# Softmax weighting with V as the stationary operand in four column tiles, row sums spread by DMA

## The chip, the cores and the metric

The kernel runs on one core of a Trainium2 chip. The metric is the device time of one execution in microseconds (us). Engines: PE (TensorE, matrix products into PSUM), DVE (VectorE), ACT (ScalarE), POOL (GpSimd) and SP, which here only issues DMAs.

## The reference, cut to what matters

```python
xn = layernorm(x)                                # x: 2048 x 640, bf16
q, k, v = xn @ wq, xn @ wk, xn @ wv              # 32 heads of 20, in 4 segments of 512 rows
for s in range(4):
    p = softmax(qs @ ks.T * 20 ** -0.5 + causal mask)
    a_dot = p @ vs
    a_mem = (phi(qs) @ M) / (phi(qs) @ z + 1e-6)      # memory of the earlier segments
    o = g * a_mem + (1 - g) * a_dot                   # g = sigmoid(beta), one per head
    M, z = M + phi(ks).T @ vs, z + phi(ks).sum()
s = concat(o) @ wo
glu = (sigmoid(xn @ w_gate) * (xn @ w_up)) @ w_down
out = x + s * silu(glu)
```

## The kernel before

The program is emitted segment by segment (n = 0 to 3), and each segment in 20 **slots**: four pairs of head groups (a group is 4 heads), five slots to a pair (`UNITS`). In a slot `scores` multiplies up to 512 columns of K by Q for 4 heads, in four row tiles of 32 partitions, into one PSUM tile `Sps`; ACT takes the exponential into `pt` (keys on partitions, queries along the row), POOL zeroes what lies over the diagonal. One slot later (two for the second half of unit 2) `weigh` multiplies by V.

`weigh` (L534) holds a 128x128 block of `pt` stationary and streams the 21 columns of one head's V: 20 values and a 1, so that column 20 of the result is the softmax's row sum. A group needs ten blocks times four heads, 40 matmuls, into one PSUM tile `A` (queries on partitions; one buffer, `ps_a`). After the group's last block DVE takes the reciprocal of the row sums (L553), multiplies it by 1 - g (L554) and multiplies the group into `od` (L556). At the start of the next segment `o_ready` adds the memory's part `om` (L468) and turns `od` by DMA transposes into `oT` (L475), which `o_proj` (L502) multiplies by Wo: five chunks of 128 rows. `mem_read` (L410 to L418) makes `om`.

The order of the work is written out by a planner. `at(time, cost, fn)` puts a task at a time that is counted in slots; `later` puts one behind the current task. The feed-forward part (`gate` L428, `up` L438, `down` L456) is a list `bulk`, from which `fill` takes as much as evens out the slots, with PE costs in us from `PASS` and the tasks' own. In a slot come `scores`, 0.45 of the slot's bulk, the due `weigh` passes, and the rest. The last four `down` passes are kept for the end, and in the tail `o_last` turns the last chunk on PE. All matmul results but `Sps` and `A` share three PSUM buffers (`ps_d`), which DVE or ACT empties. Each engine works in the order of emission, and so does SP with its DMAs: a DMA that waits holds all behind it. V, K, Q of the next segment (`v_tile` L360, `k_chunk` L289, `q_chunk` L321), the bound of the scores (`q_bound` L334, five matmuls of 32 columns in four column tiles) and the relays of K and Q through DRAM (L274, L310, L353) are tasks of the same planner, and so are the transposes of phi(K), `pkt` (L378).

Of the kernel before, what the change touches and what calls it, by code (L numbers as in the profile page):

```python
# [9 lines left out]
P = 128  # L10
S = 2048
D = 640
H = 32
DH = 20
VW = DH + 1
KR = DH + 4
NSEG = 4
# [36 lines left out]
FIRST = 0.45  # L54
PASS = [0.41, 0.41, 0.41, 0.2, 0.61]
R = NSLOT / 24
# [3 lines left out]
def kernel(  # L60
# [31 lines left out]
    Ks = [dpool.tile([D, L], BF, name=f"Ks{i}") for i in range(2)]  # L92
    Cs = [dpool.tile([4, H, L], BF, name=f"Cs{i}") for i in range(2)]

    ctx.enter_context(tc.manual_schedule(engines={ENG.PE, ENG.Activation, ENG.DVE, ENG.Pool, ENG.SP}))
# [24 lines left out]
    def empty(fn):  # L120
        pending.append((seq[0], fn))
        if not delay[0]:
            flush()

    def later(lag, fn, *a):
# [43 lines left out]

    def load_late(name, src):  # L170
        parts = src.shape[0] // P
        W[name] = cpool.tile([P, parts, D], BF, name=f"W{name}")
        nc.scalar.dma_start(W[name][:], src.rearrange("(f p) n -> p f n", p=P))

# [6 lines left out]
                            base=0, pattern=[[-1, P]], channel_multiplier=1)  # L181
    V = []
    for i in range(8):
        va = cpool.tile([P, H, VW], BF, name=f"va{i}")
        V.append(va)
    QT = [cpool.tile([P, 4, L], BF, name=f"QT{i}") for i in range(3)]
    KT = [cpool.tile([P, 4, L], BF, name=f"KT{i}") for i in range(3)]
    nInd = cpool.tile([P, DC, H], F32, name="nInd")
    BD = cpool.tile([P, DC, HW, VW], BF, name="BD")
    Mbd = cpool.tile([P, DC, HW, VW], BF, name="Mbd")  # L190

    def v_ones(a, b):
        for i in range(a, b):
            nc.gpsimd.memset(V[i][:, :, DH:VW], 1.0)

    def make_ind():
# [16 lines left out]

    gin = {}

    def gates():
# [185 lines left out]
    def mem_read(n, j, b):  # L402
        s = st[n]
        if j == 0 and b == 0:
            s["om"] = opool.tile([P, 4, D], BF, name="om", bufs=1)
        am = dtile([P, 16, VW], F32, "am")
        parts = [c for c in range(DC) if H0[c] < 16 * b + 16 and H1[c] > 16 * b]
        for i, c in enumerate(parts):
            lo, hi = max(H0[c], 16 * b), min(H1[c], 16 * b + 16)
            nc.tensor.matmul(am[:, lo - 16 * b:hi - 16 * b, :].rearrange("p h e -> p (h e)"),  # L410
                             lhsT=s["q5"][:, c, j * P:(j + 1) * P],
                             rhs=Mbd[:, c, lo - H0[c]:hi - H0[c], :].rearrange("p h e -> p (h e)"),
                             start=(i == 0), stop=True, skip_group_check=True)
        rm = opool.tile([P, 16], F32, name="rm", bufs=3)
        nc.vector.scalar_tensor_tensor(out=rm[:], in0=am[:, :, DH], scalar=1e-6,
                                       in1=gin["ginv"][:, 16 * b:16 * b + 16], op0=ALU.add, op1=ALU.mult)
        nc.vector.reciprocal(rm[:], rm[:])
        nc.vector.tensor_tensor(  # L418
            s["om"][:, j, b * HB:(b + 1) * HB].rearrange("p (h e) -> p h e", e=DH),
            am[:, :, 0:DH], rm[:].unsqueeze(2).to_broadcast([P, 16, DH]), op=ALU.mult)  # L420

# [42 lines left out]

    def o_add(n, j, c0, c1):
        o = st[n]["od"][:, j, c0:c1]
        if n >= 1:
            nc.vector.tensor_tensor(o, o, st[n]["om"][:, j, c0:c1], op=ALU.add)  # L468

    def o_turn(n, j, parts):  # L470
        if "oT" not in st[n]:
            st[n]["oT"] = fpool.tile([P, 4, DC, P], BF, name="oT", bufs=1)
        dst = st[n]["oT"][:, j, 0:parts, :]
        src = st[n]["od"][:, j, 0:parts * P]
        later(0.7, lambda: nc.sync.dma_start_transpose(dst, src))  # L475

    def o_ready(n, j, parts=DC):
        o_add(n, j, 0, parts * P)
        o_turn(n, j, parts)

    def o_last(n):
        po = dtile([P, 4, P], BF, "po")
        for j in range(4):
            nc.tensor.transpose(po[:, j, :], st[n]["od"][:, j, (DC - 1) * P:D], ident[:])
        nc.scalar.copy(st[n]["oT"][:, :, DC - 1, :], po[:])

# [8 lines left out]
    def o_proj(n, j, half):  # L495
# [5 lines left out]
        for c in range(DC):  # L501
            nc.tensor.matmul(sp[:], lhsT=s["oT"][:, j, c, :], rhs=W["o"][:, c, hs],  # L502
                             start=(c == 0), stop=(c == DC - 1))
# [29 lines left out]

    def weigh(n, pair, u, dg, pt):  # L534
        s = st[n]
        g = 2 * pair + dg
        first = (u, dg) in ((0, 0), (2, 1))
        if first:
            s["A"] = ps_a.tile([P, 4, 4, VW], F32, name="Aps")
        A = s["A"]  # L540

        mine = [(kb, c0) for (d, kb, c0, ncol) in UNITS[u] if d == dg]
        blocks = [(kb, c0 + (qb - kb) * P, qb) for (kb, c0) in mine for qb in range(kb + 1, 4)]
        blocks += [(kb, c0, kb) for (kb, c0) in mine]
        for (kb, off, qb) in blocks:
            for r in range(4):
                nc.tensor.matmul(A[:, qb, r, :], lhsT=pt[:, r, off:off + P],  # L547
                                 rhs=V[4 * (n % 2) + kb][:, 4 * g + r, :],
                                 start=first, stop=True, skip_group_check=True)
                first = False  # L550
        if (u, dg) in ((2, 0), (4, 1)):
            rd = opool.tile([P, 4, 4], F32, name="rd", bufs=3)
            nc.vector.reciprocal(rd[:], A[:, :, :, DH])  # L553
            nc.vector.tensor_tensor(rd[:], rd[:], gin["omg"][:, 4 * g:4 * g + 4].unsqueeze(1).to_broadcast([P, 4, 4]),  # L554
                                    op=ALU.mult)
            nc.vector.tensor_tensor(  # L556
                s["od"][:, :, 4 * g * DH:(4 * g + 4) * DH].rearrange("p q (r e) -> p q r e", e=DH),
                A[:, :, :, 0:DH], rd[:].unsqueeze(3).to_broadcast([P, 4, 4, DH]), op=ALU.mult)

# [13 lines left out]
    def startup():  # L573
# [33 lines left out]
        make_bd()  # L607
        v_ones(4, 8)
        take(1)
        relay(0, 0, Qs, QT)  # L610
# [5 lines left out]
        ln_stats(1, 1, 0, 1)  # L616
        gates()
        take(1)
        ln_norm(1, 0, 0)
# [13 lines left out]

    startup()
    at(6.8, 0, load_late, "d", B_w_down)
    at(10.2, 0, load_late, "o", A_wo)


    for n in range(NSEG):
        w = NSLOT * n  # L640
        m = n + 1
        if m < NSEG:
# [7 lines left out]
            for c in range(DC):  # L650
                at(w + R * (8.8 + 1.0 * c), 1.08, k_chunk, m, c)
                at(w + R * (13.8 + 1.1 * c), 1.08, q_chunk, m, c)
                if m + 1 < NSEG:
                    at(w + R * (12.8 + 0.85 * c), 0.0, phi, m, "k5", c)
                at(w + R * (18.3 + 0.8 * c), 0.0, phi, m, "q5", c)
# [7 lines left out]
            for i, cs in enumerate(([0, 1, 2], [3, 4])):  # L663
                at(w + R * (10.0 + 3.2 * i), 0.75 - 0.25 * i, m_update, n, cs)
        if n >= 1:
            for j in range(4):
                at(w + R * (1.1 + 0.3 * j), 0.0, o_ready, n - 1, j)
                at(w + R * (4.0 + 0.5 * j if j < 3 else 9.6), 0.0, xr_load, n - 1, j)
            for i in range(8):
                at(w + R * (5.4 + 1.1 * i), 0.68, o_proj, n - 1, i // 2, i % 2)  # L670
                at(w + R * (3.4 + 0.85 * i), 0.25, mem_read, n, i // 2, i % 2)

    for j in range(4):
        at(NSLOT * NSEG - 8 + 0.5 * j, 0.0, xr_load, NSEG - 1, j)
        at(NSLOT * NSEG - 0.9 + 0.2 * j, 0.0, o_ready, NSEG - 1, j, DC - 1)

# [10 lines left out]

    due, held = [], []
    for n in range(NSEG):
        st[n]["od"] = opool.tile([P, 4, D], BF, name="od")  # L690
        if n:
            bulk += [(1.09, fn, (n, f)) for f in range(FC) for fn in (gate, up)]
        bulk += [(1.64, down, (n, j, h)) for j in range(4) for h in range(2)]
        keep = 4 if n >= NSEG - 2 else 0

# [20 lines left out]
        for slot in range(NSLOT):  # L716
            pair, u = divmod(slot, NU)
            now = NSLOT * n + slot
            share = max(level - fixed[slot], 0.0)
            pt = scores(n, pair, u)  # L720
            delay[0] = True
            goal += FIRST * share
            fill(now + 0.45, (tasks,))
            for w in due:
                weigh(*w)
            delay[0] = False
            flush()
            while first and first[0][0] < now + 1.0:
                run_task(first)
            due, held = held, []  # L730
            due.append((n, pair, u, UNITS[u][0][0], pt))
            if u == 2:
                held.append((n, pair, u, 1, pt))
            goal += (1.0 - FIRST) * share
# [5 lines left out]

    cost, fn, a = bulk.pop(0)
    fn(*a)
    for w in due:
        weigh(*w)
    drain()
    n = NSEG - 1
    for j in range(4):
        o_add(n, j, (DC - 1) * P, D)
    for i, (cost, fn, a) in enumerate(bulk):
        if i == len(bulk) - 1:  # L750
            o_last(n)
        fn(*a)
    for j in range(4):
# [32 lines left out]
```

## Time and profile before

| | |
|---|---|
| median of 3 runs | 341.0 us (340.95 to 342.18) |
| the profiled execution | 342.2 us, span 340.5 us |
| instructions | 8352 |
| weighting, L547 | 1280 matmuls, 44.6 us busy; as many weight loads, 43.3 us |
| first scores of the four segments and of the last slot | 32.8, 103.1, 185.2, 260.2 and 321.0 us |
| DMA | 35.5 MB in 54725 packets, 104 GB/s on average |

A line of the page's groups reads: line, engine, operation, output<-inputs, shapes, count | busy us, mean ns of one | idle time of the engine before them and what ended it. A line of the timeline reads: start in us from the span's start, duration, engine, line, operation, count. The slices show the busy share in tenths, in 40 equal parts of the span. Matmuls are pipelined: PE's pace is read from starts, not from durations.

### The profile page before, as it was taken

Reading aid. Unit: us, or ns where it says so; the run is one execution under the profiler, and the core shown is the slowest. Engines: PE = TensorE matmul, PEld = TensorE weight load, DVE = VectorE, ACT = ScalarE, POOL = GpSimd, SP = SyncE. Lnnn points to the kernel's source line nnn. Section 1 sums busy time; section 2 is a strip of 40 time slices with the busy share of each in tenths; the row PEclk is TensorE's granted clock in tenths of the full one; section 3 lists DMA queues with packets and bytes.
Section 4 is the critical chain, followed back from the end, with each engine's and each line's share of the span. In section 5 each row is a group of like instructions: output and inputs, shape, how many; then the busy total and the mean of one; then the engine's idle time right before and its main releaser. Section 6 shows DMA issues by size and latency. Waiting matters only on the chain.

```text
span 340.5 us, 8352 instructions
## 1 busy us (share of the span) xinstructions
PE 330.1 (97%) x3402; PEld 186.8 (55%) x3402; DVE 223.6 (66%) x533; ACT 225.7 (66%) x236; POOL 111.5 (33%) x157
## 2 busy tenths in 40 slices
PE   8999899999999999999999999999999999999995
PEld 7543455545664565554466456554456655544673
DVE  6375366769786577778758867885655677633455
ACT  3652797688886666477686765565887775786730
POOL 6645232222245222332235312323222323233214
PEclk9999999999999999999999999999999999999999
DMA  7953984665822621045720461042220521110032
GB/s 237 339 182 108 329 130 87 229 212 125 185 74 37 120 74 45 19 137 93 218 72 2 87 127 40 21 154 80 79 69 3 84 74 40 58 60 2 3 62 77
DMA packets 54725, 35.53 MB, mean 104 GB/s; under 512 B 28576, under 2 KB 54688, under 8 KB 54688
## 3 DMA queue, kind: packets, MB, share of 16 engines
q1 hardware_dynamic: 52480, 32.23, 36.5%
q10 hardware_dynamic: 2208, 2.79, 2.5%
q8 instruction: 26, 0.43, 0.5%
q14 instruction: 11, 0.09, 0.1%
HBM read 20.19 MB, written 8.39 MB: 84 GB/s over the span
## 4 chain that ended last, share of the span: by engine, by line
PE 83%; DMA 6%; DVE 6%; ACT 2%; POOL 1%; issue 1%; SPq 1%; DVEq 0%; ACTq 0%; POOLq 0%
PE up L438 14%; PE gp L428 14%; PE yp L456 11%; PE Aps L547 8%; PE Sps L522 6%; PE psk L289 6%; PE sp L502 6%; PE psv L360 6%; PE psq L321 6%; DMA Cs<-cb 2%; DMA Wu<-in_B_w_up_dram 2%; PE wps L571 2%; DMA xnT<-xn 1%; PE dm L388 1%; DMA Qs<-q 1%; PE am L410 1%
## 5 line engine op out<-in xcount | busy, mean ns | idle before, releaser
L527 ACT ACTIVATE pt<-Sps 128x2048 bf16<-128x2048 f32 x80 | 150.2, 1877 | 28.9 <-PE Sps L522 26.1
L530 POOL TENSOR_SCALAR_AFFINE_SELECT pt<-pt 128x1024 bf16<-128x1024 bf16 (+1 forms) x80 | 75.7, 947 | 196.7 <-ACT pt L527 196.7
L428 PE MATMUL gp<-xnT,Wg 128*128 128x512 bf16 x240 | 59.7, 379 | 1.1 <-DMA Wg<-in_B_w_gate_dram 0.6
L438 PE MATMUL up<-xnT,Wu 128*128 128x512 bf16 x240 | 59.7, 380 | 0.2 <-DMA Wu<-in_B_w_up_dram 0.2
L456 PE MATMUL yp<-Wd,hT 128*128 128x320 bf16 x384 | 57.1, 299 | 0.0
L442 DVE SCALAR_TENSOR_TENSOR hT<-tg,up 128x512 bf16<-128x512 bf16 x48 | 32.7, 682 | 30.4 <-PE up L438 27.4
L431 ACT ACTIVATE tg<-gp 128x512 bf16<-128x512 f32 x48 | 28.6, 597 | 35.9 <-PE gp L428 35.9
L547 PEld LDWEIGHTS <-pt 128*128 128x128 bf16 x1280 | 43.3, 96 | 14.7 <-DVE od L556 1.4
L547 PE MATMUL Aps<-va,pt 128*128 128x21 bf16 x1280 | 44.6, 173 | 0.9 <-DVE od L556 0.7
L456 PEld LDWEIGHTS <-hT 128*128 128x128 bf16 x384 | 35.3, 97 | 15.3 <-issue 2.4
L438 PEld LDWEIGHTS <-Wu 128*128 128x128 bf16 x240 | 21.2, 97 | 24.6 <-issue 3.5
L522 PE MATMUL Sps<-QT,KT 24*128 24x128 bf16 (+3 forms) x512 | 32.6, 301 | 1.4 <-ACT pt L527 0.7
L428 PEld LDWEIGHTS <-Wg 128*128 128x128 bf16 x240 | 21.0, 97 | 22.9 <-issue 2.1
L461 DVE SCALAR_TENSOR_TENSOR aa<-t,yp 128x320 bf16<-128x320 bf16 x32 | 15.2, 482 | 19.5 <-ACT t L459 19.3
L360 PE MATMUL psv<-Wv,xnT 128*128 128x320 bf16 x160 | 26.4, 300 | 0.8 <-ACT tg L431 0.5
L459 ACT ACTIVATE t<-yp 128x320 bf16<-128x320 f32 x32 | 14.0, 437 | 19.2 <-PE yp L456 18.0
L502 PE MATMUL sp<-Wo,oT 128*128 128x320 bf16 x160 | 25.9, 300 | 0.0
L522 PEld LDWEIGHTS <-KT 24*128 24x128 bf16 x512 | 9.5, 92 | 27.0 <-issue 25.9
L321 PE MATMUL psq<-xnT,Wq 128*128 128x512 bf16 x100 | 24.3, 380 | 0.0
L289 PE MATMUL psk<-xnT,Wk 128*128 128x512 bf16 x100 | 24.3, 380 | 0.0
L504 DVE SCALAR_TENSOR_TENSOR aa<-aa,sp 128x320 bf16<-128x320 bf16 x32 | 15.5, 485 | 8.5 <-PE sp L502 8.4
L553 DVE RECIPROCAL rd<-Aps 128x16 f32<-128x16 f32 x32 | 8.1, 254 | 16.4 <-PE Aps L547 16.4
(74 smaller groups left out, 333.6 us busy)
## 6 DMA issues: line engine op xcount, KB each, us to landing
KT<-Ks SPq DMA_DIRECT2D x32, 80.0 KB
QT<-Qs SPq DMA_DIRECT2D x32, 80.0 KB
xr<-in_A_x_dram SPq DMA_DIRECT2D x15, 160.0 KB
out_dram<-xr SPq DMA_DIRECT2D x15, 160.0 KB
xt<-in_A_x_dram SPq DMA_DIRECT2D x6, 320.0 KB
Wg<-in_B_w_gate_dram SPq DMA_DIRECT2D x3, 640.0 KB
Wu<-in_B_w_up_dram SPq DMA_DIRECT2D x3, 640.0 KB
Wd<-in_B_w_down_dram ACTq DMA_DIRECT2D x1, 1920.0 KB
```

Of the source, the lines that this page charges most:

```text
L289: nc.tensor.matmul(ps[:], lhsT=W["k"][:, k, c * P:(c + 1) * P], rhs=s["xnT"][:, k, :], start=(k == 0), stop=(k == DC - 1))
L321: nc.tensor.matmul(ps[:], lhsT=W["q"][:, k, c * P:(c + 1) * P], rhs=s["xnT"][:, k, :], start=(k == 0), stop=(k == DC - 1))
L360: nc.tensor.matmul(ps[:], lhsT=s["xnT"][:, k, j * P:(j + 1) * P], rhs=W["v"][:, k, half * HB:(half + 1) * HB], start=(k == 0), stop=(k == ...
L428: nc.tensor.matmul(gp[:], lhsT=Wg[f // 4][:, k, fo:fo + P], rhs=s["xnT"][:, k, :], start=(k == 0), stop=(k == DC - 1))
L438: nc.tensor.matmul(ps[:], lhsT=Wu[f // 4][:, k, fo:fo + P], rhs=s["xnT"][:, k, :], start=(k == 0), stop=(k == DC - 1))
L442: empty(lambda: nc.vector.scalar_tensor_tensor(out=h[:], in0=tg[:], scalar=1.0, in1=ps[:], op0=ALU.add, op1=ALU.mult))
L456: nc.tensor.matmul(yp[:], lhsT=s["hT"][f][:, j * P:(j + 1) * P], rhs=W["d"][:, f, hs], start=(f == 0), stop=(f == FC - 1))
L502: nc.tensor.matmul(sp[:], lhsT=s["oT"][:, j, c, :], rhs=W["o"][:, c, hs], start=(c == 0), stop=(c == DC - 1))
L522: nc.tensor.matmul(Sps[:, r, c0:c0 + ncol], lhsT=kt[32 * r:32 * r + KR, gi, kb * P:(kb + 1) * P], rhs=qt[32 * r:32 * r + KR, gi, kb * P:L] ...
L527: nc.scalar.activation(pt[:], Sps[:], ACT.Exp, scale=SCALE)
L530: nc.gpsimd.affine_select(out=diag, in_=diag, compare_op=ALU.is_ge, fill=0.0, base=0, pattern=[[0, 4], [0, cnt], [1, P]], channel_multipli ...
L547: nc.tensor.matmul(A[:, qb, r, :], lhsT=pt[:, r, off:off + P], rhs=V[4 * (n % 2) + kb][:, 4 * g + r, :], start=first, stop=True, skip_grou ...
```

## The change

V becomes the stationary operand: 32 columns from a head's place in V (21 of its own, the rest of the next heads', or ones) in the column tile of that head, and `pt` is streamed, up to 512 columns at once, so a group has 16 matmuls in four column tiles. The result has the heads' values on partitions: partitions 32r to 32r+19 are head r's output, 32r+20 is its row sum, and the 11 others hold nothing of use. The passes come due two slots later (three for the second half of unit 2) and are emitted at the head of a slot, right before `scores`.

A whole group is copied from PSUM by one operation, into `oa` (groups 0 to 2) or `ob` (groups 3 to 7). `divide` sends the row sums through DRAM, so that they lie on 128 partitions, inverts them, multiplies by 1 - g (`oc`, made by `columns` with the masks of `make_sel`), sends them back through DRAM to 20 partitions a head (`rdb`), and `scale` multiplies. Groups 0 to 2 then go through DRAM (`spill`, `fill_holes`) into the 12 free partitions of each head in `ob`, so that Wo is needed in five chunks of 128 rows; Wo is put in that order through DRAM (`wo_gather`, `wo_load`), and `mem_read` writes `om` in that order too, with four multiplications for the first half, and transposes it by DMA. For the last two groups of the last segment `spread` copies the row sums to their partitions with a matmul by `sel`, and inverts 128x512 at once. Some tasks move in time.

```diff
-PASS = [0.41, 0.41, 0.41, 0.2, 0.61]
+PASS = [0.32, 0.21, 0.21, 0.21, 0.11]
+NA = 3
...
+    def wo_gather():
+        W["o"] = cpool.tile([P, DC, D], BF, name="Wo")
+        for r in range(4):
+            nc.sync.dma_start(Wx[r], wo_rows[r][:, 0:NA, :])
+
+    def wo_load(r):
+        nc.sync.dma_start(W["o"][32 * r:32 * r + DH, :, :], wo_rows[r][:, NA:NG, :])
+        nc.sync.dma_start(W["o"][32 * r + DH:32 * r + 32, :, :],
+                          Wx[r].rearrange("e g n -> (e g) n").rearrange("(c x) n -> x c n", c=DC))
...
+        lo = 4 * NA if b == 0 else 16
         nc.vector.tensor_tensor(
-            s["om"][:, j, b * HB:(b + 1) * HB].rearrange("p (h e) -> p h e", e=DH),
-            am[:, :, 0:DH], rm[:].unsqueeze(2).to_broadcast([P, 16, DH]), op=ALU.mult)
+            om[:].rearrange("p (h x) -> p h x", x=32)[:, lo - 4 * NA:16 * b + 16 - 4 * NA, 0:DH],
+            am[:, lo - 16 * b:16, 0:DH],
+            rm[:, lo - 16 * b:16].unsqueeze(2).to_broadcast([P, 16 * b + 16 - lo, DH]), op=ALU.mult)
+        if b == 0:
+            holes = om[:].rearrange("p (c r x) -> p r c x", c=DC, r=4)
+            for g in range(NA):
+                nc.vector.tensor_tensor(
+                    holes[:, :, :, DH + g::NA],
...
+            return
...
+        later(0.8, lambda: nc.sync.dma_start_transpose(dst, om[:]))
...
+    def divide(n, g0, g1, col, time):
...
+        def den_out():
+            for a, b in spans(g0, g1):
+                nc.sync.dma_start(Ds[:, a - g0:b - g0, :], rows_of(n, a, b)[DH::32])
+
+        def den_in():
+            nc.sync.dma_start(dn[:], Ds.rearrange("r g (k x) -> (r g k) x", x=16 * cnt))
+
+        def invert():
+            nc.vector.reciprocal(rc[:], dn[:])
+            nc.vector.tensor_scalar(rb[:], rc[:], oc[:, col:col + 1], None, op0=ALU.mult)
+
+        def rec_out():
+            nc.sync.dma_start(Rs.rearrange("r g (k x) -> (r g k) x", x=16 * cnt), rb[:])
+
+        def rec_in():
+            for r in range(4):
+                nc.sync.dma_start(rdb[32 * r:32 * r + DH, 0:cnt, :], Rs[r].partition_broadcast(DH))
+
+        def scale(a, b):
+            o = rows_of(n, a, b)
+            nc.vector.tensor_tensor(o, o, rdb[:, a - g0:b - g0, :], op=ALU.mult)
+
+        soon(time + 0.1, den_out)
+        soon(time + 0.75, den_in)
+        soon(time + 1.5, invert)
+        soon(time + 1.55, rec_out)
+        soon(time + 2.2, rec_in)
+        for g in range(g0, g1):
+            soon(time + 2.9 + 0.25 * (g - g0), scale, g, g + 1)
...
+    def fill_holes(n, c0, c1):
+        for r in range(4):
...
+            nc.sync.dma_start(st[n]["ob"][32 * r + DH:32 * r + 32, c0:c1, :], rows[:, c0:c1, :])
+
+    def spread(n, g, col):
+
+        o = st[n]["ob"][:, g - NA, :]
+        ps = dtile([P, L], F32, "dps")
+        nc.tensor.matmul(ps[:], lhsT=sel[:], rhs=o, start=True, stop=True)
+        nc.vector.reciprocal(ps[:], ps[:])
+        nc.vector.scalar_tensor_tensor(out=o, in0=o, scalar=oc[:, col:col + 1], in1=ps[:],
+                                       op0=ALU.mult, op1=ALU.mult)
...
+        for (d, kb, c0, ncol) in UNITS[u]:
+            if d != dg:
+                continue
             for r in range(4):
-                nc.tensor.matmul(A[:, qb, r, :], lhsT=pt[:, r, off:off + P],
-                                 rhs=V[4 * (n % 2) + kb][:, 4 * g + r, :],
-                                 start=first, stop=True, skip_group_check=True)
-                first = False
...
+                h = 4 * g + r
+                nc.tensor.matmul(A[32 * r:32 * r + 32, kb * P:L],
+                                 lhsT=Vw[4 * (n % 2) + kb][:, h * VW:h * VW + 32], rhs=pt[:, r, c0:c0 + ncol],
+                                 start=first, stop=True, skip_group_check=True, tile_position=(0, 32 * r))
+            first = False
...
+        (nc.scalar.copy if now >= NSLOT * NSEG else nc.vector.tensor_copy)(rows_of(n, g, g + 1).rearrange(
+            "p g n -> p (g n)"), A[:])
+        last = n == NSEG - 1
+        if g == 3:
+            divide(n, 0, 4, 0, now)
+            soon(now + 3.9, spill, n)
+        elif g == 7 and not last:
+            divide(n, 4, 8, 1, now)
+            soon(now + 0.3, fill_holes, n, 0, DC)
+            soon(now + 2.9, o_add, n, 0)
+        elif g == 5 and last:
+            divide(n, 4, 6, 2, now)
+            soon(now + 0.5, fill_holes, n, 0, 3)
...
+        elif g == 6 and last:
+            soon(now + 0.4, spread, n, 6, 3)
+            soon(now + 0.6, fill_holes, n, 3, 4)
+            soon(now + 0.95, o_add, n, 3)
...
-        keep = 4 if n >= NSEG - 2 else 0
+        keep = {NSEG - 2: 4, NSEG - 1: 5}.get(n, 0)
...
+            passes(now)
             pt = scores(n, pair, u)
+            due.append((now + 2, (n, pair, u, UNITS[u][0][0], pt)))
...
+    take(1)
+    passes(NSLOT * NSEG + 1)
     drain()
...
+    take(1)
+    spread(n, 7, 4)
+    fill_holes(n, 4, 5)
+    take(len(bulk))
+    o_add(n, 4)
     for j in range(4):
         for h in range(2):
             o_proj(n, j, h)
```

## The prediction

> **What bounds the kernel now.** I read the summary and the slices first: they say which engine could set the end.
>
> ```profile
> PE 330.1 (97%) x3402; PEld 186.8 (55%) x3402; DVE 223.6 (66%) x533; ACT 225.7 (66%) x236; POOL 111.5 (33%) x157
> PE   8999899999999999999999999999999999999995
> PEclk9999999999999999999999999999999999999999
> ```
>
> PE is busy in every slice and its clock is full. A busy PE need not be at its peak, so next comes the timeline of PE alone, where starts tell the pace.
>
> ```profile
> 162.83 0.75 PE L547 MATMUL Aps<-va,pt 128*128 128x21 bf16 x24
> 163.43 1.24 PE L428 MATMUL gp<-xnT,Wg 128*128 128x512 bf16 x5
> 164.60 0.40 PE L522 MATMUL Sps<-QT,KT 24*128 24x512 bf16 x4
> 164.93 1.25 PE L321 MATMUL psq<-xnT,Wq 128*128 128x512 bf16 x5
> ...
> 243.76 0.55 PE L547 MATMUL Aps<-va,pt 128*128 128x21 bf16 x16
> 244.24 0.60 PE L334 MATMUL cps<-aq,IK 128*32 128x512 bf16 x5
> 244.78 0.40 PE L522 MATMUL Sps<-QT,KT 24*128 24x128 bf16 x8
> 245.11 1.25 PE L438 MATMUL up<-xnT,Wu 128*128 128x512 bf16 x5
> ```
>
> Three things are read here. 24 weighting matmuls take 163.43 - 162.83 = 0.60 us, 25 ns each, and the next group follows at the same pace. Full 512-column matmuls are 0.216 us apart (five in 1.24, of which the last one's own 0.38 overlaps what follows). And each change of the array's shape costs something: from the first gp at 163.43, five of 0.216 end at 164.51, the scores start at 164.60; their 0.216 of streaming ends at 164.82, psq starts at 164.93. So some **0.095 us a change**. Beyond these paces PE's starts leave only some 5 us of stalls between 45 and 330 us, half of it next to weighting passes. So a nanosecond taken from PE is a nanosecond gained, unless another engine then holds it up. The timeline of the tail shows that there is no pause at the end to hide anything in: after the last scores at 321.02 one group follows the other until the output.
>
> ```profile
> 321.97 3.42 PE L456 MATMUL yp<-Wd,hT 128*128 128x320 bf16 x24
> 325.22 0.55 PE L547 MATMUL Aps<-va,pt 128*128 128x21 bf16 x16
> 325.63 3.42 PE L456 MATMUL yp<-Wd,hT 128*128 128x320 bf16 x24
> 328.88 0.39 PE L484 MATMUL po<-ident,od 128*128 128x128 bf16 x4
> 329.11 1.79 PE L456 MATMUL yp<-Wd,hT 128*128 128x320 bf16 x12
> 330.74 5.60 PE L502 MATMUL sp<-Wo,oT 128*128 128x320 bf16 x40
> ```
>
> Last, the groups by shape, for what VectorE will be asked to do.
>
> ```profile
> L553 DVE RECIPROCAL rd<-Aps 128x16 f32<-128x16 f32 x32 | 8.1, 254 | 16.4 <-PE Aps L547 16.4
> L224 DVE RECIPROCAL ginv<-gcol 128x32 f32<-128x32 f32 x1 | 0.3, 339 | 0.0
> L415 DVE SCALAR_TENSOR_TENSOR rm<-am,ginv 128x16 f32<-128x16 f32 x24 | 4.0, 168 | 2.1 <-PE am L410 2.1
> L323 DVE CAST q<-psq 128x512 bf16<-128x512 f32 x15 | 10.3, 688 | 8.0 <-PE psq L321 7.9
> L556 DVE TENSOR_TENSOR od<-Aps,rd 128x320 bf16<-128x320 f32 x32 | 15.7, 491 | 1.1
> ```
>
> **1. The weighting passes on PE: -13.2 us.** Before: 1280 matmuls x 25 ns = 32.0. After: for each of 32 head groups four chunks (512, 384, 256 and 128 columns), each as four matmuls in four column tiles. Whether such tiles run together is shown by cps: its first four matmuls lie in four column tiles with 512 columns, and all five have 0.60 us, which is one matmul's 0.39 and 0.21 more: the fifth, in the first one's tile, starts about 0.22 after the first. So the four cost what one does. A chunk costs columns/512 x 0.216 and about 0.01 for the staggered starts: 0.22 + 0.17 + 0.12 + 0.07 = 0.59 a group, 18.8 in all.
> The Trainium skill (TensorE: Matmul & The Clock Gate, Measured speedup vs the span model) gives 3.07x, not 4x, for four row tiles of 512 columns; by that the passes would take 32 x 1280 x 4 columns / 2.4 GHz / 3.07 = 22 us, an estimate, and 3.4 of the gain would go. The 0.22 us from first to fifth matmul speaks against it here.
>
> **2. One more change of shape in each slot: +7.8 us.** Before, the weighting had the bulk's 128*128 shape and went in without a seam (162.83 to 163.43). After, the slot begins bulk to column tiles, column tiles to row tiles, row tiles to bulk: three changes where there were two. The new one is column to row, and cps to Sps shows it: first cps 244.24, 0.43 for two rounds, Sps at 244.78, so 0.10 over. 80 slots x 0.095 = 7.6, and 0.2 for the last pass, which has no scores behind it. The two sel matmuls (0.43) replace four transposes (0.22): +0.2. PE's own work: **-13.2 + 7.8 + 0.2 = -5.2 us**.
>
> **3. VectorE gets more work and waits: +3.0 us.** Out: 32 x (0.254 + 0.257 + 0.491) = 32.1 us of L553 to L556, and the od additions, 7. In: 31 copies of 128x512 out of PSUM at 0.688 = 21.3; 30 products by rdb at 0.42 (the od addition of 128x512 has 419 ns) = 12.6; 15 additions of omT, 6.3; eight inversions of 64 or 32 columns, 0.7 each = 5.5; in 12 reads of the memory four small operations of some 0.25 for one of 0.49, +6; columns(), 2; the two wide reciprocals with their products, 8 (below). Net +22 us, some 4 in each segment. The windows view has VectorE busy 16.94 of 20 us at 139 to 159 and 16.31 of 20 at 178 to 198; there the two divisions of a segment fall (slots 11 to 15, and 1 to 5 of the next), each adding about 2.3: over 90%. VectorE runs in order, and now waits for DMAs: `invert` for dn, the products for rdb. Queued behind them are the evacuations of up, V and k that give PE its three ps_d buffers. A dependent DMA was issued 2.6 us after its source (Ks at 222.53, KT at 225.17), and four relays took 1.46 us to issue. So den_out, den_in, invert, rec_out and four rec_in take about 1.9 + 1.6 + 0.7 + 1.6 + 3 us from the copy's end to the product, where the plan has 2.9 slots of 3.9 us less the copy's 1.5: about even, until SP stands at a pkt transpose (L378 waited up to 3.6 us for VectorE, and issues for 1.2) ahead of rec_in. SP's load itself (20 issues of 0.4 in, four transposes out per segment) is small beside its idle time. Lower end: PE feels none of it and the 2.4 us that it lost around the old passes go, -2.4; upper end, six divisions with two waits of 0.7 each passed on whole, +8.5. I take +3.0, nearer to the lower end, since two free buffers cover 2 us of a stall. Startup: make_sel is some 5 us of POOL behind 30 us, where it waited 5.9 before its first mask at 36.5; nothing. Wo by a copy in DRAM: nothing, it is needed 80 us later.
>
> **4. The tail: +5.5 us.** The last two groups divide by `spread`: sel matmul, a reciprocal of 128x512, a product, four DMAs (fill_holes), an addition, then the projection's chunk. The trace has no such reciprocal. From 16 to 32 columns it rises by 85 ns and it stands 85 over the ordinary operation of 16: about 6.1 ns a column, so 0.16 + 512 x 6.1 = **3.3 us**; the other end is the copy of that shape, 0.69. I take 3.3. From the end P of the last passes: copy on ScalarE under one down pass (1.64); sel at P+1.9; behind that pass's evacuation VectorE starts the reciprocal at P+2.9, done P+6.2, product P+6.9, four DMAs 3.3 (1.46 of issue and the landing), P+10.2, addition P+10.6. PE has 1.64 + 0.3 + 3 x 1.64 + 0.54 (four of five chunks) = 7.4. It is 3.2 short. For group 6 the same 4.0 us of VectorE stand in slot 79 ahead of the down passes' evacuations, and o_add(3) then holds them again for its DMAs; one buffer is sel's, so PE runs about one pass further: some 2.3 lost. Ends: 0.6 with the short reciprocal; 9 if the rdb products of groups 4 and 5 (slots of 3.0 us there, a chain of 11) come late as well.
>
> **The sum.** The profiled execution has 342.2 us (span 340.5, 1.7 around it); the runs' median is 341.0, 1.2 less. 342.2 - 5.2 + 3.0 + 5.5 = 345.5, and as a median **344.3 us**, +1.0%. The bounds: -5.2 - 2.4 + 0.6 gives 334.0; -5.2 + 8.5 + 9 gives 353.3.
>
> **Rivals.**
> A, it pays: VectorE keeps up, and the tail's reciprocal is short or covered. For it: VectorE waits for PE 27 us before hT alone, and is nearly idle from 305 to 321 (5.51 of 16). Against: the slope of the two reciprocals. 341.0 - 5.2 - 0.5 + 1 = 336.3. Chance 0.27.
> B, a little of each, the gain and the tail cancel: 341 within 1.7. Chance 0.20.
> Forecast, 342.7 to 347.5: chance 0.33.
> C, slower by VectorE's waits for DMA: place, the rdb product at the end of a division's third slot; price, 0.7 to 1.5 us each time for 12 waits; it decides from a wait of over two PE tiles (2.2 us), when no free buffer is left. 341.0 - 5.2 + 8.5 + 5.5 = 349.8. Chance 0.12.
> D, a pause of PE in the tail slows its clock. In the empty start 40 matmuls of 128 columns took 4.45 us, 0.106 apart; po's four are 0.056 apart. A cold stretch as long as that first one loses 2.2 us: 344.3 + 2.2 = 346.5. The Trainium skill (TensorE: Matmul & The Clock Gate, HAM oscillation) has the clock halved after about 3.4 us of idleness; no run here shows that. The pauses worked out above are 1.5 to 3 us. Chance 0.06.
> E, the column tiles run one after another: 1280 x 4 x 32 columns at 0.216 per 512 are 69 us, +50: 394. cps speaks against it. Chance 0.02.
>
> **How the numbers follow.** Faster by over 0.5%: A, 0.27. Within 0.5% (about what this measurement can tell from no change): B, 0.20. Slower: the forecast, C, D and E, 0.53. The range leaves out the ends of A and of C, and E: 335.5 to 350.5.
>
> **What would show it.** Aps matmuls of 128*32 in fours, a 512 chunk 0.22 from the next (1); Sps 0.31 after the last Aps of 512 columns (2); idle time of VectorE put down to DMA dn and rdb, idle time of PE put down to VectorE in slots 12 to 15 (3); a RECIPROCAL of 128x512 at 3.3 us twice, and PE gaps of 1.5 to 3 us after 320 us (4). If that reciprocal takes under 1 us, the forecast falls to A; if the gaps stand in the body and not in the tail, C is right.

## The result and the profile after

The changed kernel takes 383.1 us (380.3 to 385.5) against 341.1 before: ratio 1.122, 95% interval 1.113 to 1.131. Forecast were 344.3 us and a range of 335.5 to 350.5. The direction was right, the size was not: 42 us instead of 3. In e4, e5 and e9 below one of each run's four executions was slow, and their times and ratios leave it out.

The summary and the clock's slices of the changed kernel (its slowest execution, 385.5 us, span 383.8 us) show the difference at once: PE is busy for 336.0 us against 330.1 before, but that is 88% instead of 97% of the span, and its clock now dips.

```profile
PE 336.0 (88%) x2599; PEld 166.3 (43%) x2632; DVE 241.4 (63%) x563; ACT 227.3 (59%) x236; POOL 114.8 (30%) x175
PE   8998996995989989998999989898999599969865
PEclk9999998897999999999999989999999899989899
```

The list of waits of the same profile (who waited for whom: total us, times, longest) says for what:

```profile
PE Aps L658 <- DVE ob L668: 11.9, 6, 4.1
DVE ob L565 <- DMA rdb<-Rs: 10.4, 3, 5.1
DVE oa L565 <- DMA rdb<-Rs: 9.1, 4, 4.1
PE Aps L658 <- DVE oa L668: 6.5, 4, 3.3
DVE k L326 <- DMA pkt<-k: 6.4, 1, 6.4
DVE rc L553 <- DMA dn<-Ds: 5.9, 2, 3.1
DVE ob L565 <- DMA xr<-in_A_x_dram: 5.0, 1, 5.0
```

L565 is `scale`, L553 `invert`, L668 the copy of a group out of PSUM. (The line with xr is rdb too: the wait ended at 301.26, and the transfer that `scale` needs came in beside xr.) VectorE stood 30 us before dn and rdb, and PE 18 us before copies that were behind. One such place follows, in the timelines of SP, VectorE and PE. (SPq is the issue of a DMA; Ds and Rs are the DRAM buffers of the row sums and of their inverses, Os that of the spilled groups.)

```profile
287.67 0.53 SPq L547 DMA_DIRECT2D Ds<-ob  x1
289.56 1.54 SPq L588 DMA_DIRECT2D ob<-Os  x4
291.14 0.36 SPq L550 DMA_DIRECT2D dn<-Ds  x1
295.02 0.34 SPq L557 DMA_DIRECT2D Rs<-rb  x1
296.46 1.42 SPq L561 DMA_DIRECT2D rdb<-Rs  x4
```

```profile
301.26 0.43 DVE L565 TENSOR_TENSOR ob<-ob,rdb 128x512 bf16<-128x512 bf16 x1 [4.96 <-DMA xr<-in_A_x_dram]
301.60 0.75 DVE L580 TENSOR_TENSOR ob<-ob,omT 128x512 bf16<-128x512 bf16 x2
302.27 0.68 DVE L668 CAST oa<-Aps 128x512 bf16<-128x512 f32 x1
```

```profile
295.86 1.25 PE L491 MATMUL gp<-xnT,Wg 128*128 128x512 bf16 x5
298.45 1.24 PE L501 MATMUL up<-xnT,Wu 128*128 128x512 bf16 x5 [1.34 <-ACT tg L494]
303.01 0.83 PE L658 MATMUL Aps<-pt,va 128*32 128x256 bf16 x8 [3.32 <-DVE oa L668]
303.78 0.61 PE L634 MATMUL Sps<-QT,KT 24*128 24x512 bf16 x4
```

The row sums leave at 287.67, and their inverses are usable at 301.26. VectorE waits 4.96 us in its order; the copy that empties `A` stands behind the waiting product and two additions, and the next pass needs `A`. PE starts no matmul from 299.3 to 303.0, and then a batch of 4 scores takes 0.61 us where it took 0.40: the clock has gone to half. A wait of VectorE of 1.92 us was enough for a pause of 4.12 us on PE, since the pass needed `A` before that wait began, and two operations on phi(K) stood between the product and the copy:

```profile
90.42 0.43 DVE L565 TENSOR_TENSOR oa<-oa,rdb 128x512 bf16<-128x512 bf16 x1 [1.92 <-DMA rdb<-Rs]
91.69 0.68 DVE L668 CAST ob<-Aps 128x512 bf16<-128x512 f32 x1
92.42 0.83 PE L658 MATMUL Aps<-pt,va 128*32 128x256 bf16 x8 [4.12 <-DVE ob L668]
```

The windows view, over stretches that begin in the pauses or just behind them, gives the clock (the column before the DMA share):

```profile
63.60:70.40 6.80, 5.50 (x23) 1.77 (x24) 4.13 (x7) 1.88 (x1) 0.42 (x1) 0.50 0.19 67
90.90:97.70 6.80, 5.28 (x24) 2.04 (x24) 5.21 (x12) 1.88 (x1) 0.68 (x1) 0.50 1.17 192
224.00:227.40 3.40, 3.35 (x16) 1.92 (x14) 3.30 (x12) 2.10 (x2) 0.84 (x1) 0.51 0.00 0
302.60:306.00 3.40, 2.99 (x19) 1.11 (x19) 3.30 (x10) 1.50 (x1) 0.00 (x0) 0.51 0.02 5
340.10:343.50 3.40, 3.40 (x9) 1.02 (x7) 0.33 (x1) 2.11 (x2) 0.68 (x1) 0.50 0.29 116
357.20:360.60 3.40, 3.40 (x15) 1.90 (x13) 3.37 (x5) 0.24 (x1) 0.07 (x1) 0.50 0.02 5
```

PE is busy for 23.9 of these 27.2 us at half clock; at full clock that work would take about half as long, so an estimate of 12 us is the clock's in this execution. Five of the six stretches follow a wait of a division. The first follows another pause: PE stood 3.14 us until 64.68 behind the copy of K, which waited 6.4 us for pkt (the list's fifth line). Where nothing waits, the passes do what was worked out. The next lines show PE in a quiet slot, then the tail: its first pause is still behind an rdb product (of groups 4 and 5), the other two belong to the tail's own division, with its reciprocal.

```profile
192.95 0.40 PE L658 MATMUL Aps<-pt,va 128*32 128x128 bf16 x8
193.28 0.40 PE L634 MATMUL Sps<-QT,KT 24*128 24x512 bf16 x4
193.61 3.43 PE L519 MATMUL yp<-Wd,hT 128*128 128x320 bf16 x24
...
356.83 0.38 PE L594 MATMUL dps<-ob,sel 128*128 128x512 bf16 x1 [2.72 <-DVE ob L668]
357.05 5.09 PE L519 MATMUL yp<-Wd,hT 128*128 128x320 bf16 x24
...
366.46 3.42 PE L519 MATMUL yp<-Wd,hT 128*128 128x320 bf16 x24 [1.67 <-DVE aa L524]
370.92 1.79 PE L519 MATMUL yp<-Wd,hT 128*128 128x320 bf16 x12 [1.04 <-DVE ob L596]
```

```profile
358.59 3.36 DVE L595 RECIPROCAL dps<-dps 128x512 f32<-128x512 f32 x1
```

### The profile page after: what moved, and what is told of

It reads as the page before. It is cut to its first block, busy times and chain, and to the rows that moved or that the text cites. A ratio compares the mean times of both kernels' runs of the same rounds, so it can differ in the third digit from the quotient of the medians.

```text
span 383.8 us, 6989 instructions
## 1 busy us (share of the span) xinstructions
PE 336.0 (88%) x2599; PEld 166.3 (43%) x2632; DVE 241.4 (63%) x563; ACT 227.3 (59%) x236; POOL 114.8 (30%) x175
## 4 chain that ended last, share of the span: by engine, by line
PE 37%; DVE 29%; DMA 20%; SPq 6%; issue 5%; ACT 2%; DVEq 0%; ACTq 0%
PE up L501 6%; PE gp L491 6%; DMA rdb<-Rs 5%; PE yp L519 5%; PE psk L337 4%; PE Aps L658 4%; PE sp L614 3%; PE Sps L634 3%; PE psv L408 3%; DMA Rs<-rb 3%; SPq L561 2%; PE psq L369 2%; DMA pkt<-k 2%; DMA Ds<-ob 2%; DVE ob L668 2%
## 5 line engine op out<-in xcount | busy, mean ns | idle before, releaser
L501 PE MATMUL up<-xnT,Wu 128*128 128x512 bf16 x231 | 60.9, 389 | 6.9 <-DVE k L326 3.1
L519 PE MATMUL yp<-Wd,hT 128*128 128x320 bf16 x384 | 58.3, 308 | 2.9 <-DVE aa L524 1.7
L505 DVE SCALAR_TENSOR_TENSOR hT<-tg,up 128x512 bf16<-128x512 bf16 x48 | 32.8, 682 | 38.1 <-PE up L501 22.1
L658 PE MATMUL Aps<-pt,va 128*32 128x128 bf16 (+3 forms) x512 | 33.3, 312 | 18.5 <-DVE ob L668 11.9
L519 PEld LDWEIGHTS <-hT 128*128 128x128 bf16 x384 | 37.4, 101 | 25.4 <-issue 9.7
L501 PEld LDWEIGHTS <-Wu 128*128 128x128 bf16 x240 | 22.4, 99 | 35.1 <-issue 11.4
L491 PEld LDWEIGHTS <-Wg 128*128 128x128 bf16 x240 | 22.5, 100 | 28.4 <-issue 5.4
L658 PEld LDWEIGHTS <-va 128*32 128x32 bf16 x512 | 10.6, 95 | 46.0 <-issue 43.2
L614 PE MATMUL sp<-Wo,ob 128*128 128x320 bf16 x160 | 26.5, 303 | 3.3 <-DVE om L475 1.0
L614 PEld LDWEIGHTS <-ob 128*128 128x128 bf16 x160 | 14.7, 99 | 13.0 <-issue 4.1
L408 PEld LDWEIGHTS <-xnT 128*128 128x128 bf16 x160 | 15.0, 99 | 10.3 <-issue 3.0
```

What stands on the lines that cost most here:

```text
L408: nc.tensor.matmul(ps[:], lhsT=s["xnT"][:, k, j * P:(j + 1) * P], rhs=W["v"][:, k, half * HB:(half + 1) * HB], start=(k == 0), stop=(k == ...
L491: nc.tensor.matmul(gp[:], lhsT=Wg[f // 4][:, k, fo:fo + P], rhs=s["xnT"][:, k, :], start=(k == 0), stop=(k == DC - 1))
L501: nc.tensor.matmul(ps[:], lhsT=Wu[f // 4][:, k, fo:fo + P], rhs=s["xnT"][:, k, :], start=(k == 0), stop=(k == DC - 1))
L505: empty(lambda: nc.vector.scalar_tensor_tensor(out=h[:], in0=tg[:], scalar=1.0, in1=ps[:], op0=ALU.add, op1=ALU.mult))
L519: nc.tensor.matmul(yp[:], lhsT=s["hT"][f][:, j * P:(j + 1) * P], rhs=W["d"][:, f, hs], start=(f == 0), stop=(f == FC - 1))
L614: nc.tensor.matmul(sp[:], lhsT=s["ob"][:, c, j * P:(j + 1) * P], rhs=W["o"][:, c, hs], start=(c == 0), stop=(c == DC - 1))
```

## The experiments

Theory W: VectorE waits in its order for the row sums' transfers; the single buffer `A` and the three `ps_d` buffers hand this on to PE. Rivals: L, VectorE has too much work; P, the column passes or their place are slow. Each time stands against the kernel before on the same chip (341.1 to 341.8 us).

| run | us | ratio to before | 95% interval |
|---|---|---|---|
| changed kernel | 383.1 | 1.122 | 1.113 to 1.131 |
| e1_nowait | 359.4 | 1.050 | 1.045 to 1.054 |
| e2_nodiv | 351.8 | 1.029 | 1.026 to 1.033 |
| e3_late | 366.7 | 1.075 | 1.069 to 1.080 |
| e4_norecip | 378.1 | 1.105 | 1.098 to 1.111 |
| e5_memold | 355.5 | 1.042 | 1.038 to 1.047 |
| e6_notail | 351.9 | 1.029 | 1.026 to 1.032 |
| e7_all | 352.1 | 1.031 | 1.028 to 1.035 |
| e8_later | 366.1 | 1.072 | 1.067 to 1.077 |
| e9_spread | 353.4 | 1.035 | 1.032 to 1.038 |
| e10_actcopy | 370.5 | 1.085 | 1.081 to 1.089 |
| e11_actall | 343.5 | 1.008 | 1.005 to 1.010 |
| e12_full | 360.7 | 1.059 | 1.052 to 1.066 |
| e13_actspread | 351.2 | 1.030 | 1.024 to 1.036 |
| e14_pool | 372.6 | 1.089 | 1.084 to 1.095 |
| e15_whole | 359.8 | 1.051 | 1.048 to 1.054 |
| e16_apart | 346.5 | 1.013 | 1.011 to 1.016 |

**e1_nowait: the same work and transfers, no wait**

```diff
-            nc.vector.reciprocal(rc[:], dn[:])
+            nc.vector.reciprocal(rc[:], W["k"][:, 0, 0:16 * cnt])
...
-            nc.vector.tensor_tensor(o, o, rdb[:, a - g0:b - g0, :], op=ALU.mult)
+            nc.vector.tensor_tensor(o, o, W["k"][:, 0:b - a, 0:L], op=ALU.mult)
```

> The changed kernel with the same operations and the same transfers, but VectorE does not read what the transfers bring: invert takes its numbers from a slice of Wk in place of dn, and the products take a slice of Wk of the same shape in place of rdb (so the output is not divided by the row sums). Theory W (VectorE stands in order before dn and rdb, some 30 us in all, holds A and the PSUM buffers, and PE's pauses then also halve its clock): nearly all of it goes in the body; what is left is the tail and the late pkt, so 345 to 353 us. Rival L (VectorE has simply too much work): at most 5 us less than the changed kernel, 376 to 383. Rival P (the column passes at the head of the slot are themselves slow): the same, 378 to 383.

359.4 us, 23.7 less. W holds and L and P fall as main causes: VectorE is as busy as in the changed kernel (243.0 us against 241.4). The expectation was still 6 us too low. One thing differs besides the edit: e1's profile has no wait for pkt. That wait differs between runs whose edits do not touch it: e3 and e4 have 4.2 and 4.1 us of it without a stretch at half clock behind it, e5 has 6.1 with one, e6 has none. So a few us of the 23.7 may be pkt's; the lowest times of the two kernels, 380.3 and 357.5, are 22.8 apart. The list of waits of e1 has no dn and no rdb any more; what is left of PE's waits for A is

```profile
PE Aps L658 <- DVE ob L668: 4.6, 3, 2.1
```

**e2_nodiv: no division but in the tail** (the `soon` lines of `divide` left out, except that of the additions)

> The changed kernel without the division by row sums for all but the last two groups: no den_out, den_in, invert, rec_out, rec_in and no products, so the output is left undivided there. The passes, the copies, the holes and the tail stay. W: 2 to 5 us under the run without the waits, 342 to 349. L: 18 us of VectorE's work are gone, so about 360 to 368. P: 375 to 383.

351.8 us, 7.6 less than e1, and the clock stayed full in the profiled execution (mean 1.000). So the division's 18 us of work on VectorE and its transfers cost more than the 2 to 5 expected, which rival L can claim, and 10 us over the kernel before had another cause.

**e3_late and e8_later: the products later, all work kept**

```diff
-            soon(time + 2.9 + 0.25 * (g - g0), scale, g, g + 1)
+            soon(time + 2.9 + lag + 0.2 * (g - g0), scale, g, g + 1)
...
-    at(6.8, 0, load_down)
+    at(8.0, 0, load_down)
```

(`lag` is 1.0 in e3, where the last line is not changed, and 2.2 for the first division of segments 0 to 2 in e8; it is 0 for groups 4 and 5 of the last segment. The smaller moves named in the expectations are left out here.)

> The changed kernel with all its work, but the products by rdb and the additions behind them come one slot (about 3.9 us) later, invert and what follows it 0.3 slots later, and the projection starts 0.8 slots later; the division of groups 4 and 5 of the last segment stays as it was. W: waits of 1.5 to 5 us become 0 to 1.5, so 353 to 363 us. L and P: no difference, 380 to 384.

> The whole computation, with the first division of a segment 2.2 slots later (1 slot in the last segment), the second 1 slot later, the projection 0.8 slots later, and the load of Wd at slot 8.0 in place of 6.8, so that it does not run into the last transposes of phi(K). Theory W: the waits left in the run with one slot's delay were 14 us of VectorE's time, of which 5 to 7 in the body go, and 3 of Wd: 358 to 363. If one slot's delay had taken all that delay can take: 365 to 368.

366.7 and 366.1 us. One slot takes 16 us away, so W holds again, though e3 stayed 4 us above its range. e8 came out as its second reading has it: 2.2 slots and a later Wd brought nothing that can be measured. In e8 the first divisions of segments 0 to 2 wait no more; the waits for dn (7.0 us), for rdb in the second divisions and in the last segment (3.8 and 3.4) remain. That the projection's place leaves no room to put these off further was not tried.

**e4_norecip: the tail without its reciprocals** (`nc.vector.reciprocal(ps[:], ps[:])` left out)

> The changed kernel without the two reciprocals of 128x512 in the tail (the last two groups are multiplied by the row sums instead of divided). They were measured at 3.36 us each. If both stand on the path that sets the end: 375 to 378 us. If the tail is hidden behind the down passes: 382 to 384.

378.1 us, some 5 less; the intervals of the two ratios leave 2 to 3 us either way on each. So a good part of their 6.7 us stands on the path, and how much exactly this run can't tell.

**e5_memold, e6_notail, e7_all: two more suspects taken out of e1**

```diff
-            for g in range(NA):
-                nc.vector.tensor_tensor(holes[:, :, :, DH + g::NA], ...
+            om[:, b * HB:(b + 1) * HB].rearrange("p (h e) -> p h e", e=DH),
+            am[:, :, 0:DH], rm[:].unsqueeze(2).to_broadcast([P, 16, DH]), op=ALU.mult)
...
     def spread(n, g, col):
+        return
-    fill_holes(n, 4, 5)
```

> The run without the waits, with mem_read's first half written by one multiplication of 128x320, as before the change, in place of one of 128x80 and three into the holes (so the memory's part stands in the wrong order). If the four small operations hold mem_read's PSUM buffer and PE with it, as the trace's idle time of PE before L459 says: 3 to 7 us less, 352 to 356. If they only fill VectorE's spare time: 358 to 360.

> The run without the waits, and without the tail's division: spread does nothing, and the holes of the last two chunks are not filled, so the last two groups are neither divided nor complete. The tail's own pauses were 6 us with a cold clock behind them: 350 to 353. If the tail's price lies in the order of the last down passes: 358 to 360.

> Both of the other two edits on the run without the waits. If the three causes (waits for transfers, mem_read's four operations, the tail) are all there is, PE's own 5.2 us of gain must come out, less some 3 us for VectorE's other work: 337 to 345. If a fourth cause is left, 346 to 352.

355.5, 351.9 and 352.1 us. The tail costs 7.5 (e6 against e1). The memory's four operations cost 3.9 by these times, 2.5 by the ratios, which is hardly clear of the noise, and nothing that can be measured once the tail is gone (e7 against e6). A fourth cause is left, as the last expectation's second half has it. The trace of e7 has PE waiting for A's copies and for the late pkt:

```profile
DVE k L326 <- DMA pkt<-k: 5.5, 1, 5.5
PE Aps L651 <- DVE ob L661: 4.8, 4, 2.1
PE up L493 <- DVE k L326: 2.3, 1, 2.3
```

**e10_actcopy and e11_actall: A's copies on ScalarE, in the whole kernel and in e7 (there with Wd at 8.0)**

```diff
-        (nc.scalar.copy if now >= NSLOT * NSEG else nc.vector.tensor_copy)(rows_of(n, g, g + 1).rearrange(
+        nc.scalar.copy(rows_of(n, g, g + 1).rearrange(
             "p g n -> p (g n)"), A[:])
```

> The changed kernel, whole, with one edit: all copies out of A go to ScalarE (0.59 us each) in place of VectorE. VectorE then still waits for the transfers, but A no longer hangs on it. If A is what passes VectorE's waits on to PE: 362 to 371 us. If the ps_d buffers pass them on just as well: 374 to 382.

> The run with all three causes taken out (352 us), with the copies out of A on ScalarE and the load of Wd at slot 8.0. Theory Y: the 5 us of pauses before passes go, and 2 of Wd: 342 to 346. Theory X: Wd's 2 us and a little for 20 us less of VectorE's work: 347 to 350.

370.5 us (12.6 less): PE's waits for copies of A on VectorE, 18.4 us, are gone, while VectorE still waits 33 us for dn and rdb. So A passed a good part of VectorE's waits on; the rest goes through the other buffers. The edit also takes 31 copies, 21 us of work, off VectorE, and what share of the 12.6 this has is not separated. And 343.5 us (8.5 less than e7): with waits, tail, memory order, A's copies and Wd all out of the way, the change is still 0.8% slower than before. In its trace PE has no wait for Aps left; new is one for ScalarE:

```profile
PE Sps L627 <- ACT pt L632: 2.6, 3, 1.6
PE cps L382 <- DVE aq L372: 2.4, 2, 2.1
```

**e9_spread, e12_full, e13_actspread: the memory's reads further apart**

```diff
-                at(w + 5.2 + 0.6 * i, 0.25, mem_read, n, i // 2, i % 2)
+                at(w + 5.2 + 0.85 * i, 0.25, mem_read, n, i // 2, i % 2)
```

> The run with all three causes taken out (352 us), with one edit: mem_read's eight tasks of a segment 0.85 slots apart in place of 0.6, ending at slot 11.2 in place of 9.4. What is left there is 10 us over the kernel before, where PE's own work is 5 us less. Theory X, the tasks that VectorE must empty (memory, projection, V and K of the next segment) crowd in slots 5 to 10: 3 to 6 us less, 346 to 349. Theory Y, the group's copy out of A at the head of each slot waits in VectorE's order: no difference, 351 to 353.

> The whole computation with all that helped and leaves it whole: products one to 2.2 slots later, Wd at 8.0, mem_read's tasks 0.85 slots apart, copies out of A on ScalarE. From the later version's 366: 5 for A, 3 to 5 for the crowding: 355 to 360 us, still over the kernel before, by the tail and by VectorE's remaining waits. If it came under 345, the tail would not cost what its own run said.

> The run without waits, memory order, tail and with the copies on ScalarE (343.5 us), and now with mem_read's tasks 0.85 slots apart. If the pauses that are left between am, sp and psv come from crowding, they go now that A no longer hides them: 339 to 341.5 us, at or under the kernel before. If not: 343 to 345.

353.4, 360.7 and 351.2 us. These three are spoiled as tests of crowding: the last two reads of a segment come after the first half of its memory update (slot 10.2; the second half is at 11.5), so they read updated memory, and PE waits for it. The list of waits of e13:

```profile
PE am L459 <- POOL Mbd L448: 4.3, 6, 1.7
```

**e14_pool: the waits for rdb on GpSimd** (`end` stands for groups 4 and 5 of the last segment)

```diff
-            nc.vector.tensor_tensor(o, o, rdb[:, a - g0:b - g0, :], op=ALU.mult)
+            (nc.vector if end else nc.gpsimd).tensor_tensor(o, o, rdb[:, a - g0:b - g0, :], op=ALU.mult)
```

> The whole computation, every wait kept, but the waits for rdb stand on GpSimd: it does the products (but for groups 4 and 5 of the last segment), ScalarE copies A, Wd is loaded at slot 8.0, invert comes 0.4 slots later, the second division's additions wait until slot 5.9 and the projection until 6.3. Theory W, it is the engine that waits which matters, not the length of the transfers: GpSimd's masks have two slots to spare, so 349 to 356 us, of which 7 are the tail. If the transfers themselves hold the kernel, or GpSimd's masks come late: 360 to 372.

372.6 us, just over the second reading. GpSimd waits instead, longer, and is in order too: its masks then come late for the passes, and the additions for the projection. It also needs 1.15 us for a product that takes VectorE 0.42, some 33 us for all 28, so this run does not separate the wait from the slower work.

```profile
POOL oa L565 <- DMA rdb<-Rs: 24.1, 4, 9.9
POOL ob L565 <- DMA rdb<-Rs: 11.3, 2, 6.6
PE sp L617 <- DVE ob L583: 7.0, 9, 1.1
PE Aps L661 <- POOL pt L645: 6.7, 4, 3.7
```

So W is better put differently: it does not matter that it is VectorE that waits, but the round trip is longer than the room that the plan leaves between the copy and the product. That the waits vanish in e8's first divisions, which have 2.2 slots more room, fits this.

**e15_whole and e16_apart: the two without that fault** (e15: e8 with A's copies on ScalarE; e16: e11 with the reads at 4.2 + 0.7 i and the projection 0.75 apart)

> The whole computation: products one to 2.2 slots later, Wd at 8.0, copies out of A on ScalarE, and the memory's reads where the change has them. (In the full version of the earlier call and in the two others with reads 0.85 slots apart, the last reads of a segment fell behind the memory's update at slots 10.2 and 11.5, read the updated memory and waited for GpSimd; in the GpSimd version the last read did.) Against that full version's 360.7: the 1.8 us pauses before two reads go, and some small ones, 352 to 357 us. If the reads' place was not what cost time there: 359 to 362.

> The run without waits, memory order and tail, with the copies on ScalarE (343.5 us), its memory reads moved to slots 4.2 to 9.1 (0.7 apart, all ahead of the memory's update) and its projection tasks 0.75 apart in place of 0.65. If the small pauses around am, sp and psv (some 3.6 us in its trace) come from crowding: 340.5 to 342.5. If spreading them does not help: 343 to 345.

359.8 and 346.5 us. e15 comes out as its second reading has it: against e12's 360.7 the place of the reads costs nothing that can be measured, while e13, with the same late reads, is 7.7 us over e11; why they cost there and not here is open. The best whole version of the change is 5% slower than the kernel before. And the small pauses of e11 are not cured by spreading: e16, above both of its ranges, took 3 us more.

## Why the prediction was wrong, point by point

- **Step 1 (passes, -13.2 us): right.** A chunk of 128 and one of 384 columns, the change to row tiles included, take 0.33 us (192.95 to 193.28): 0.07 + 0.16 + 0.10. The column tiles run together.
- **Step 2 (one more change of shape, +7.8 us): right.** Over the 78 places where Sps follows Aps without a wait of PE's, the starts leave 0.101 us each, 7.9 in all.
- **Step 3 (VectorE's work and waits, +3.0): this step failed**, and its upper end of 8.5 too. The runs give 23.7 us for the waits with the clock behind them (e1; a few of them may be pkt's), and 8.5 for A's copies on VectorE and Wd's load (e11 against e7). The term for VectorE's work was not too small: 22 us more were forecast, 17.8 measured (241.4 against 223.6). Three parts of the waits were wrong. (a) The round trip was put at 8.8 us after the copy; it took 301.26 - 287.67 = 13.6 from the first issue, and the copy had ended just before. In the second division of a segment `fill_holes` stands between den_out and den_in on SP (1.5 us of issue, not counted), dn needed 3.0 here instead of 1.6 (291.14 to 294.15, where VectorE had waited 3.15 us for it), and the four broadcasts of rdb 4.8 instead of 3 (3.9 to 4.9 in the seven divisions of four groups). With slots of 3 to 4 us the plan's 2.9 slots did not cover it. (b) "Two free buffers cover 2 us of a stall" named the wrong buffer: `A` is a single one, its copy stands behind the waiting product, and the pass at the head of the next slot needs it. e10, which cuts this edge and takes the copies off VectorE, gains 12.6 us. (c) A pause costs more than its length where half clock follows it, and step 3 had no term for this.
- **Rival C** had the mechanism and the place, with 12 waits of 0.7 to 1.5 us; the 10 measured ones were 1.4 to 5.1 us, and it did not take 2.2 us to decide: the one of 1.92 us went with 4.12 us of pause on PE. **Rival D** had the clock, but only in the tail and for one cold stretch; there were six. The Trainium skill (TensorE: Matmul & The Clock Gate, HAM oscillation) has the throttle come back after about 3.4 us without work. The four longest pauses, at 61, 88, 299 and 335 us, are 3.1 to 4.1 us of idle PE and have half clock behind them, which comes close to it. But half clock also followed pauses of 1.8 us (from 221.0 to 222.85) and 2.7 us (ended at 356.83), so here shorter ones were enough; and it did not follow pauses of 1.8 and 1.7 us in the same trace (ended at 114.40 and 180.31) or one of 2.3 us in e7 (ended at 63.29). The length of a pause alone does not decide, and what else does is open.
- **Step 4 (tail, +5.5): right in its mechanism.** The reciprocal of 128x512 took 3.36 us against the 3.3 forecast; the tail cost 7.5 (e6). The two differences that the forecast names give 85/16 = 5.3 ns a column, which would be 2.9 us; how 6.1 came of them is not worked out, so that this term fits so well is in part luck.
- **Startup and Wo, nothing: right for the start** (first scores at 32.6 us against 32.8). Not named was that the last transposes of phi(K) come late beside Wd's load: the copy of K waited 6.4 us for pkt, once. Of the ten profiles with Wd at slot 6.8, the changed kernel's among them, eight have this wait, with 3.1 to 6.6 us; of the seven with Wd at 8.0 two have it, with 1.3 and 1.4.
- **Rival A fell, and its premise too**: with the tail and all waits gone the change is at 343.5 us, not at 336. By the summary of e11 PE is busy for 322.6 us, 7.5 less than before, and idle for 19.2 instead of 10.4; among the waits are q_bound, scores that wait for ScalarE, and the projection. What makes these is not settled: spreading the tasks was tried and did not help.

## What to carry to other kernels

When a result is sent through DRAM and comes back to an engine that works in order, add up the whole trip, with every issue that stands between its legs on the same queue, and ask which single buffer is released behind the waiting instruction: here that buffer, before the pool, set how long a wait was free. Moving the wait to another engine in order does not shorten the trip, and in e14 it gained nothing. And an engine at 97% pays for a pause twice, if its clock falls behind it.

## What the runs showed of the hardware

A broadcast from DRAM to four times 20 partitions (rdb, 80 KB each) took 3.9 to 4.9 us from its first issue to its use, where the forecast had 3. A copy of 128x512 out of PSUM took 0.68 us on VectorE and 0.59 on ScalarE. A product of two bf16 tiles of 128x512 took 0.42 us on VectorE and 1.15 on GpSimd (e14). A reciprocal on VectorE took 0.55 us at 64 columns and 3.36 at 512, about 6.3 ns a column. The change of the PE array's shape from column tiles to row tiles took 0.10 us (78 places). Stretches at half the granted clock lasted 3.4 or 6.8 us.
